# Attention and two layers on one core: the transposes of the probabilities read float32 tiles instead of float32r copies

## The chip, the core and the metric

The kernel runs on one core of a Trainium2 chip. The core has a matrix engine (TensorE, in the profile PE, its weight loads PEld), three engines for elementwise work (VectorE = DVE, ScalarE = ACT, GpSimd = POOL), and a queue engine, SyncE (SP), which here issues every transfer. Work lies in SBUF, the results of TensorE in the banks of PSUM. The metric is the device time of one execution in microseconds.

## What is computed

Attention for 8 batches of 8 heads with 512 local and 32 global tokens of size 64, and behind it two layers over all 4608 tokens:

```python
k_all = np.concatenate([k_g, k_l], axis=2)
v_all = np.concatenate([v_g, v_l], axis=2)
out_g = np.matmul(sm(scale * np.matmul(q_g, k_all.transpose(0, 1, 3, 2))), v_all)
mask = np.abs(pos[:, None] - pos[None, :]) <= 32
s_ll = np.where(mask, scale * np.matmul(q_l, k_l.transpose(0, 1, 3, 2)), -1e9)
s_lg = scale * np.matmul(q_l, k_g.transpose(0, 1, 3, 2))
out_l = np.matmul(sm(np.concatenate([s_lg, s_ll], axis=-1)), v_all)
x = np.concatenate([out_g, out_l], axis=2).transpose(0, 2, 1, 3).reshape(4608, 512)
h = x @ w_in                      # 512 x 2048
return (h * (1.0 / (1.0 + np.exp(-h)))) @ w_out
```

`sm` is the softmax over the last axis. Everything is float32.

## The kernel before

**Numbers.** TensorE multiplies in the type float32r. A float32 value is split into a part that float32r holds exactly (names ending in `hi`) and the remainder (`lo`), and a product is the sum of two or three matmuls (hi with hi, hi with lo, lo with hi). ScalarE makes the `hi` parts, VectorE or GpSimd subtracts for the `lo` parts.

**Attention of the local queries.** It is cut into 128 steps: 8 batches, 4 chunks of 128 queries, 4 pairs of heads. A query sees only keys within 32 positions, so a chunk needs 192 local keys and the 32 global ones, 224 columns. A step k runs through these functions:

- `st_load`, `st_vload`: transfers of queries, keys and values into `raw` and `vraw` (L322, L324, L329).
- `st_split`, `st_vsplit`: the hi and lo parts (`qk`, `klo`, `vhi`, `vlo`).
- `st_scores`: the scores on TensorE (L369); VectorE adds the mask and finds the maximum (L373), ScalarE does the exponential (L377), VectorE the sum's reciprocal (L379, L380), and each head's half is scaled, one on ScalarE (L381), one on VectorE (L382; GpSimd for the first four steps). The probabilities of both heads stand in one tile `probs` of 128 x 512 float32, of which there are two, used in turn. Then a transfer (L385) copies `probs` bit for bit to a tile `rr` of type float32r. There is one such tile, and a second for odd steps among the first 12.
- `st_turn`: four transposes of 128 x 128 on TensorE (L393), with `rr` as the weights and the identity `ident` as the moving operand, into a bank of PSUM `t`; ScalarE and VectorE make `pt_hi` and `pt_lo` of it (L396, L397).
- `st_out`: the products with the values (L421), whose results become parts of `xh` and `xl`, the input of the layers.

**Attention of the global queries.** Once per batch, four heads are stacked on the partitions of a tile `pg` (two such tiles, `pgs`). `g_scores` writes the scores, `g_soft` does the softmax in place, `g_move` copies the tile by two transfers to float32r tiles `rg` (L296, L297; the larger one lies in a buffer of the tag `o`, which the way out of the layers uses too), and `g_turn` transposes these on TensorE (L310, L313). The transposed part goes along with the local ones as 32 more columns.

**Layers.** The tokens go through in 12 blocks of two or three tiles of 128. For each of 16 slices of the hidden size, `first_layer` does 12 matmuls (L550), then tanh on ScalarE (L556), a product on VectorE (L557) and the split (L559, L560); `second_layer` adds three matmuls per token tile (L569 to L571). In the first block the weights come in as 64-bit words and are turned into float32 and split (L225 to L239), much of it on VectorE (L233, L234, L236).

**What sets the order.** Each piece of attention has a due time, counted in steps from its scores (`DUE`, `TURN`, `HEAD` and so on: transposes 1.6 steps after the scores, 2.25 more for the first 12 steps). The pieces are sorted by it; before the first block they run by themselves, later `fill` puts those of the next block between the matmuls of the present one. TensorE keeps this written order. The order on the other engines and on SP's queue is set by a scheduler that goes by its own estimate of the times; the first loads of weights keep the order in which they are written. Each engine, and SP's queue, takes its instructions in turn: one that waits holds back those behind it.

Buffers of the first steps lie in two pools that later give their room to the last slices of the weights; `held` lists what is still in use there, and `load_weights` first runs the pieces that free it.

Of the kernel before, what the change touches and what calls it, by code (L numbers as in the profile page):

```python
# [9 lines left out]
F32 = mybir.dt.float32  # L10
F32R = mybir.dt.float32r
# [22 lines left out]
NEG = -8.0e9              # times the scale of 1/8: -1e9  # L34
SCALE = 0.125

# [1 line left out]
SIZES = [3, 2] + [3] * 9 + [2]       # token tiles in each block of the two layers  # L38
NLATE = 4                            # slices of the weights that take the place of the first buffers
# [19 lines left out]
PRE, PACE, LOOK = 0, 0.75, 1         # weights converted during the first steps  # L59
END = 0.6                            # how far the attention is ahead of a block  # L60
# [22 lines left out]
BUFS = dict(qk=[2, 2], raw=2, rr=1, p=2, vraw=2)  # L83
# [10 lines left out]
def attention_moe_kernel(ctx: ExitStack, tc: tile.TileContext, qk0_in, qk_in, v_in, gqk, wts, out):  # L94
# [7 lines left out]
    # buffers of the first steps, in two parts that later hold the last slices of the weights  # L102
# [6 lines left out]
    # until the layers start, attention has their banks too  # L109
# [12 lines left out]
    id32 = work.tile([P, P], F32R, tag="qk", bufs=BUFS["qk"][0], name="id32").bitcast(F32)  # L122
    make_identity(nc, id32)
    ident = const.tile([P, P], F32R, name="ident")
    nc.vector.tensor_copy(out=ident, in_=id32)
# [17 lines left out]
    # probabilities: columns past the window stay zero  # L143
    probs = []
    for i in range(BUFS["p"]):
        t = const.tile([P, 2, 2 * P], F32, name=f"probs{i}")
        nc.gpsimd.memset(t, 0.0)
        probs.append(t)
    pgs = [const.tile([P, SKV], F32, name=f"pg{i}") for i in range(2)]
    # transposed probabilities by unit and key tile; 32 more columns for the global queries  # L150
    # what of the first buffers is still in use
    held = [set() for _ in first]
    pts = []
# [33 lines left out]

    def rr_tile(k):
        if k % 2 and k < RRS and first[0]:
            held[0].add(f"rr{k}")  # L190
            return first_pool[0].tile([P, 4 * P], F32R, tag="rr", bufs=1, name=f"rr{k}")
        return work.tile([P, 4 * P], F32R, tag="rr", bufs=BUFS["rr"], name=f"rr{k}")

# [5 lines left out]
    def load_weights():  # L199
        f, c0 = w_next  # L200
        i = (f - (NF - NLATE)) // 2
        if f == CLOSE and not closing:
            closing.append(f)
        if i >= 0 and first[i]:
            while held[i]:
                advance(stream[done][0])
            first[i].__exit__(None, None, None)
            first[i] = None
            side = ("left", "right")[i]
            first_pool[i] = ctx.enter_context(tc.tile_pool(name=f"late{i}", bufs=1, side=side, reuse_waits="tile"))  # L210
        if c0 == 0:
            home = const if i < 0 else first_pool[i]
            w_hi.append(home.tile([P, 2 * DM], F32R, name=f"w_hi{f}"))
            w_lo.append(home.tile([P, 2 * DM], F32R, name=f"w_lo{f}"))
        n = DM if first[1] else DM // 2
        w_next[:] = (f, c0 + n) if c0 + n < 2 * DM else (f + 1, 0)
        sl = slice(c0, c0 + n)
        hi, lo = w_hi[f][:, sl], w_lo[f][:, sl]
        if first[1]:
            raw = first_pool[1].tile([P, 2 * DM], I32, tag="raw", bufs=3, name=f"raw_w{f}_{c0}")  # L220
            w = first_pool[1].tile([P, n], F32, tag="w", bufs=2, name=f"w{f}_{c0}")
        else:
# [10 lines left out]
        nc.vector.tensor_scalar(out=up, in0=wi, scalar1=3, scalar2=None, op0=ALU.logical_shift_left)  # L233
        nc.vector.scalar_tensor_tensor(out=wi, in0=wi, scalar=0x80000000, in1=up, op0=ALU.bitwise_and,  # L234
                                       op1=ALU.bitwise_or)
        nc.vector.scalar_tensor_tensor(out=wi, in0=low, scalar=29, in1=wi, op0=ALU.logical_shift_right,  # L236
                                       op1=ALU.bitwise_or)
# [21 lines left out]
    def g_scores(b, p):  # L259
        hi, lo = state.pop(("gqk", p))  # L260
        did(("scores", b, p), *([("move", b - 1, p // 2)] if b else []))
# [11 lines left out]
    # program order is the order of the data  # L273
# [18 lines left out]
    def g_move(b, hh):  # L292
        did(("move", b, hh), ("soft", b, hh))
        r0 = two.tile([P, 4 * P], F32R, tag="o", name=f"rg0_{b}_{hh}")
        r1 = two.tile([P, SG], F32R, tag="rg", name=f"rg1_{b}_{hh}")
        nc.sync.dma_start(out=r0.bitcast(F32), in_=pgs[hh][:, : 4 * P])  # L296
        nc.sync.dma_start(out=r1.bitcast(F32), in_=pgs[hh][:, 4 * P :])  # L297
        state["rg", hh] = r0, r1

    def g_turn(b, hh):  # L300
        r0, r1 = state.pop(("rg", hh))
# [6 lines left out]
        for i in range(4):  # L308
            sl = slice(i * P, (i + 1) * P)
            nc.tensor.transpose(tb[:, sl].bitcast(F32R), r0[:, sl], ident)  # L310
        nc.scalar.copy(out=pgt[:, 0:4, hs, :], in_=tb.rearrange("p (t h q) -> p t h q", t=4, h=4))
        tb = attbank("s", f"gu{b}_{hh}")
        nc.tensor.transpose(tb[:SG, :P].bitcast(F32R), r1, ident)  # L313
        nc.scalar.copy(out=pgt[:SG, 4, hs, :], in_=tb[:SG, :P].rearrange("p (h q) -> p h q", h=4))

# [39 lines left out]
    def st_scores(k, b, c, pr):  # L355
# [14 lines left out]
        p = probs[k % BUFS["p"]]  # L370
# [12 lines left out]
        # a copy that keeps every bit for the transpose  # L383
        rr = rr_tile(k)
        nc.sync.dma_start(out=rr.bitcast(F32), in_=p.rearrange("p u j -> p (u j)"))  # L385
        tiles["rr", k] = rr

    def st_turn(k, b, c, pr):
        rr = tiles.pop(("rr", k))
        free(f"rr{k}")  # L390
        t = attbank("t", f"t{k}")
        for i in range(4):
            nc.tensor.transpose(t[:, i * P : (i + 1) * P].bitcast(F32R), rr[:, i * P : (i + 1) * P], ident)  # L393
# [147 lines left out]
    def first_layer(n, f):  # L541
# [13 lines left out]
        # twice h * sigmoid(h); the half goes into the way out  # L555
# [7 lines left out]
    def second_layer(n, f, gh, gl):  # L563
# [9 lines left out]
        if f == NF - 1:  # L573
            while ("rg", 0) in state or ("rg", 1) in state:
                advance(stream[done][0])
# [26 lines left out]
def _layout(q_l, k_l, v_l, q_g, k_g, v_g, w_in, w_out):  # L602
# [26 lines left out]
    # the first steps: both heads' keys once, and each one's queries zero on the other's rows  # L629
# [9 lines left out]
    # two heads on the rows; each one's queries are zero on the other's rows  # L639
# [28 lines left out]
```

## Time and profile before

| | us |
|---|---|
| median of the runs (lowest, highest of 3) | 1108.76 (1107.52, 1111.5) |
| span of the profiled execution | 1108.1 |
| transfers, mean | 122 GB/s |
| of these: `rr` | 128 transfers of 256 KB |
| `rg` | 16 of 256 KB and 16 of 16 KB |

The page gives the profiled execution's time as its span. Busy time is the time in which an engine has an instruction running. The busy time of TensorE contains the overlap of matmuls that follow each other, so the time from start to start is the better measure of what one costs. The chain of waits follows the last instruction back, at each step to what released it.

### The profile page before, as it was taken

The numbers are of one execution on the slowest core, as the hardware profiler recorded it, in microseconds if no ns is written. First come the engines' busy times: TensorE is split into PE (matmuls) and PEld (weight loads), VectorE is DVE, ScalarE is ACT, GpSimd is POOL, SyncE is SP. The second block draws the span as 40 slices with busy tenths as digits, with TensorE's granted clock in tenths as the row PEclk, the third lists the DMA queues.
The fourth block names the chain that finished last, engine by engine and source line by source line (L and its number), as shares of the span: only waits on it lengthen the run. The fifth ranks groups of instructions, "written<-read, shape, count | busy, mean of one in ns | idle before, by whom it ended". The sixth has DMA issues, their size and how long they took to land.

```text
span 1108.1 us, 21579 instructions
## 1 busy us (share of the span) xinstructions
PE 1042.5 (94%) x6824; PEld 947.8 (86%) x6824; DVE 798.5 (72%) x2467; ACT 725.1 (65%) x1933; POOL 228.5 (21%) x441
## 2 busy tenths in 40 slices
PE   5647889999999999999999999999999999999998
PEld 4646778898999999999989999999999999889996
DVE  6989998777778867766667877777777768863322
ACT  7876676776677766766567776667666658763232
POOL 8756775321100111001010111101100011100000
PEclk8678899999999999999999999999999999999999
DMA  8576554543343443342233443334333324420000
GB/s 249 179 219 188 182 170 130 156 121 117 109 145 115 138 138 110 113 148 83 82 112 112 147 130 117 111 116 158 109 109 120 111 92 148 138 76 20 1 30 19
DMA packets 74800, 134.76 MB, mean 122 GB/s; under 512 B 10432, under 2 KB 30400, under 8 KB 74688
## 3 DMA queue, kind: packets, MB, share of 16 engines
q1 hardware_dynamic: 74688, 133.40, 38.8%
q8 instruction: 54, 0.88, 0.3%
q14 instruction: 58, 0.48, 0.1%
HBM read 86.44 MB, written 8.91 MB: 86 GB/s over the span
## 4 chain that ended last, share of the span: by engine, by line
PE 80%; DVE 10%; DMA 3%; issue 3%; ACT 3%; POOL 1%; SPq 0%; DVEq 0%; ACTq 0%; POOLq 0%
PE h L550 31%; PE out L569 11%; PE out L571 10%; PE out L570 10%; PE o L421 8%; PE s L369 4%; PE t L393 3%; DVE w L234 2%; DVE w L236 1%; DMA rr<-probs 1%; DMA raw_w<-in_wts_dram 1%; DVE raw_w L233 1%; DVE pt_lo L397 1%; ACT probs L377 1%; DVE probs L373 1%
## 5 line engine op out<-in xcount | busy, mean ns | idle before, releaser
L550 PE MATMUL h<-xh,w_hi 128*128 128x384 f32 (+1 forms) x768 | 255.6, 333 | 0.1
L550 PE MATMUL h<-xh,w_lo 128*128 128x384 f32 (+1 forms) x768 | 252.3, 329 | 0.0
L550 PE MATMUL h<-xl,w_hi 128*128 128x384 f32 (+1 forms) x768 | 252.1, 328 | 0.0
L569 PE MATMUL out<-w_hi,gh 128*128 128x512 f32 x544 | 224.8, 413 | 0.0
L571 PE MATMUL out<-w_hi,gl 128*128 128x512 f32 x544 | 215.6, 396 | 3.0 <-DVE gl L560 1.8
L570 PE MATMUL out<-w_lo,gh 128*128 128x512 f32 x544 | 214.7, 395 | 0.0
L556 ACT ACTIVATE t<-h 128x384 f32<-128x384 f32 (+1 forms) x192 | 90.5, 471 | 186.2 <-PE h L550 175.8
L404 POOL CAST pt_hi<-pgt 128x64 fp32r<-128x64 f32 (+1 forms) x160 | 50.4, 327 | 726.1 <-PE o L421 719.2
L557 DVE SCALAR_TENSOR_TENSOR t<-t,h 128x384 f32<-128x384 f32 (+1 forms) x192 | 101.6, 529 | 122.7 <-ACT t L556 121.7
L550 PEld LDWEIGHTS h<-xh,w_hi 128*128 128x128 f32 x768 | 145.4, 189 | 6.0 <-ACT xh L427 0.6
L550 PEld LDWEIGHTS h<-xl,w_hi 128*128 128x128 f32 x768 | 145.5, 189 | 5.4
L550 PEld LDWEIGHTS h<-xh,w_lo 128*128 128x128 f32 x768 | 145.3, 189 | 0.0
L560 DVE TENSOR_TENSOR gl<-t,gh 128x384 fp32r<-128x384 f32 (+1 forms) x192 | 107.3, 559 | 48.5 <-PE out L571 43.1
L571 PEld LDWEIGHTS out<-w_hi,gl 128*128 128x128 f32 x544 | 102.8, 189 | 28.4 <-DVE gl L560 4.6
L377 ACT ACTIVATE probs<-probs,st 128x224 f32<-128x224 f32 x256 | 121.4, 475 | 7.3 <-DVE st L373 6.2
L373 DVE CUSTOM_DVE_ANT_0 probs<-s,mask 128x224 f32<-128x224 f32 x256 | 89.3, 384 | 50.4 <-PE s L369 47.0
L421 PE MATMUL o<-pt_hi,vhi 128*64 128x160 f32 (+1 forms) x512 | 99.4, 238 | 20.1 <-ACT pt_hi L396 7.8
L570 PEld LDWEIGHTS out<-w_lo,gh 128*128 128x128 f32 x544 | 103.6, 190 | 11.2
L569 PEld LDWEIGHTS out<-w_hi,gh 128*128 128x128 f32 x544 | 103.2, 190 | 11.4 <-ACT gh L559 0.4
L559 ACT CAST gh<-t 128x384 fp32r<-128x384 f32 (+1 forms) x192 | 94.6, 493 | 21.2 <-DVE t L557 17.8
L421 PE MATMUL o<-pt_hi,vlo 128*64 128x160 f32 (+1 forms) x512 | 96.3, 237 | 0.0
L421 PE MATMUL o<-pt_lo,vhi 128*64 128x160 f32 (+1 forms) x512 | 79.8, 238 | 16.3 <-DVE pt_lo L397 11.8
(82 smaller groups left out, 2016.5 us busy)
## 6 DMA issues: line engine op xcount, KB each, us to landing
raw<-in_qk_dram SPq DMA_DIRECT2D x100, 352.0 KB, 3.0
rr<-probs SPq DMA_DIRECT2D x128, 256.0 KB, 2.3
vraw<-in_v_dram SPq DMA_DIRECT2D x128, 128.0 KB, 2.4
raw_w<-in_wts_dram SPq DMA_DIRECT2D x28, 512.0 KB, 4.0
raw_g<-in_gqk_dram SPq DMA_DIRECT2D x32, 304.0 KB, 2.8
out_dram<-o SPq DMA_DIRECT2D x32, 256.0 KB, 2.6
raw<-in_qk_dram SPq DMA_DIRECT2D x28, 240.0 KB, 3.6
rg<-pg SPq DMA_DIRECT2D x16, 256.0 KB, 2.4
```

Source lines behind the costliest of these rows:

```text
L373: nc.vector.tensor_tensor_reduce(out=p[:, u, :W], in0=s[:, u * W : (u + 1) * W], in1=mask_of[c], scale=-SCALE, scalar=3.0e38, op0=ALU.add, ...
L377: nc.scalar.activation(p[:, u, :W], p[:, u, :W], AF.Exp, bias=st[:, u : u + 1], scale=-1.0, accum_out=st[:, 2 + u : 3 + u])
L404: nc.gpsimd.tensor_copy(out=pt_hi[:n, :, a, P:], in_=g)
L421: nc.tensor.matmul(o[:D, u * wide : u * wide + m], v[:, a, u, :], pt[:, u, a, :m], start=(i == 0), stop=(i == len(terms) - 1))
L550: nc.tensor.matmul(h[:, :nt], wt, x[:, c, :nt], start=(i == 0), stop=(i == 3 * NCC - 1))
L556: nc.scalar.activation(t[:, :nt], h[:, :nt], AF.Tanh, scale=0.5)
L557: nc.vector.scalar_tensor_tensor(out=t[:, :nt], in0=t[:, :nt], scalar=1.0, in1=h[:, :nt], op0=ALU.add, op1=ALU.mult)
L559: nc.scalar.copy(out=gh[:, :nt], in_=t[:, :nt])
L560: nc.vector.tensor_tensor(out=gl[:, :nt], in0=t[:, :nt], in1=gh[:, :nt].bitcast(F32), op=ALU.subtract)
L569: nc.tensor.matmul(o, gh[:, sl], wh, start=(f == 0), stop=False)
L570: nc.tensor.matmul(o, gh[:, sl], wl, start=False, stop=False)
L571: nc.tensor.matmul(o, gl[:, sl], wh, start=False, stop=(f == NF - 1))
```

## The change

The transposes read the softmax's own tile, as float32. The tiles `rr` and `rg` and the transfers into them are gone, `g_move` does nothing any more, the identity is float32 (its cast on VectorE is gone), and the PSUM tiles are written as float32. The tiles of probabilities now have to last until their transposes have run, so there are three and not two; in the first 12 steps (`RRS`) there are five, of which two lie in the first of the two early pools. The scores of the global queries need the transposes of the batch before, where they needed its copies. The tail of a block no longer runs pieces of attention until `rg` is used up.

```diff
-BUFS = dict(qk=[2, 2], raw=2, rr=1, p=2, vraw=2)
+BUFS = dict(qk=[2, 2], raw=2, p=3, vraw=2)
...
-    id32 = work.tile([P, P], F32R, tag="qk", bufs=BUFS["qk"][0], name="id32").bitcast(F32)
-    make_identity(nc, id32)
-    ident = const.tile([P, P], F32R, name="ident")
-    nc.vector.tensor_copy(out=ident, in_=id32)
+    ident = const.tile([P, P], F32, name="ident")
+    make_identity(nc, ident)
...
-    for i in range(BUFS["p"]):
-        t = const.tile([P, 2, 2 * P], F32, name=f"probs{i}")
+    for i in range(BUFS["p"] + 2):
+        home = const if i < BUFS["p"] else first_pool[0]
+        t = home.tile([P, 2, 2 * P], F32, name=f"probs{i}")
         nc.gpsimd.memset(t, 0.0)
         probs.append(t)
+    probs_of = {}
...
+    held[0].update(f"p{k}" for k in range(RRS) if k % 5 >= BUFS["p"])
...
-        did(("scores", b, p), *([("move", b - 1, p // 2)] if b else []))
+        did(("scores", b, p), *([("turn", b - 1, p // 2)] if b else []))
...
     def g_move(b, hh):
         did(("move", b, hh), ("soft", b, hh))
-        r0 = two.tile([P, 4 * P], F32R, tag="o", name=f"rg0_{b}_{hh}")
-        r1 = two.tile([P, SG], F32R, tag="rg", name=f"rg1_{b}_{hh}")
-        nc.sync.dma_start(out=r0.bitcast(F32), in_=pgs[hh][:, : 4 * P])
-        nc.sync.dma_start(out=r1.bitcast(F32), in_=pgs[hh][:, 4 * P :])
-        state["rg", hh] = r0, r1
...
-            nc.tensor.transpose(tb[:, sl].bitcast(F32R), r0[:, sl], ident)
+            nc.tensor.transpose(tb[:, sl], pg[:, sl], ident)
...
-        nc.tensor.transpose(tb[:SG, :P].bitcast(F32R), r1, ident)
+        nc.tensor.transpose(tb[:SG, :P], pg[:, 4 * P :], ident)
...
-        p = probs[k % BUFS["p"]]
+        i = k % (5 if k < RRS else BUFS["p"])
+        p, probs_of[i] = probs[i], k
...
-        rr = rr_tile(k)
-        nc.sync.dma_start(out=rr.bitcast(F32), in_=p.rearrange("p u j -> p (u j)"))
-        tiles["rr", k] = rr
+        tiles["p", k] = p.rearrange("p u j -> p (u j)")
 
     def st_turn(k, b, c, pr):
-        rr = tiles.pop(("rr", k))
-        free(f"rr{k}")
+        p = tiles.pop(("p", k))
+        free(f"p{k}")
...
-            nc.tensor.transpose(t[:, i * P : (i + 1) * P].bitcast(F32R), rr[:, i * P : (i + 1) * P], ident)
+            nc.tensor.transpose(t[:, i * P : (i + 1) * P], p[:, i * P : (i + 1) * P], ident)
...
-            while ("rg", 0) in state or ("rg", 1) in state:
-                advance(stream[done][0])
```

Three places of the built programs, engine by engine; the numbers behind names tell buffers apart. Line numbers of the changed kernel differ from those before by some ten.

TensorE, in the middle of a block: the transposes of a step between the last matmul of a first layer and the second layer. Before:

```order
L550 MATMUL h_14_6298<-xh_3975,w_lo_2274 128x384
L393 MATMUL t_6318<-ident,rr_6184 128x128 x4
L569 MATMUL out_0_5328<-w_hi_2171,gh_13_6216 128x512
L570 MATMUL out_0_5328<-w_lo_2172,gh_13_6216 128x512
L571 MATMUL out_0_5328<-w_hi_2171,gl_13_6217 128x512
```

With the change:

```order
L539 MATMUL h_14_6148<-xh_3877,w_lo_2216 128x384
L382 MATMUL t_6168<-ident,probs_122 128x128 x4
L558 MATMUL out_0_5198<-w_hi_2115,gh_13_6068 128x512
L559 MATMUL out_0_5198<-w_lo_2116,gh_13_6068 128x512
L560 MATMUL out_0_5198<-w_hi_2115,gl_13_6069 128x512
```

Nothing has moved: TensorE has the same instructions in the same order all through, only the transposed tile is another.

SP's queue, from the first loads of weights on. Before:

```order
L296 DMA rg_0_0_239<-pg_124 128x512
L297 DMA rg_0_0_240<-pg_124 128x32
L322 DMA raw_423<-in_qk_dram 128x480
L296 DMA rg_0_1_249<-pg_125 128x512
L385 DMA rr_237<-probs_120 128x512
L297 DMA rg_0_1_250<-pg_125 128x32
L385 DMA rr_269<-probs_122 128x512
L225 DMA raw_w_512_434<-in_wts_dram 128x1024
L322 DMA raw_490<-in_qk_dram 128x480
L225 DMA raw_w_0_503<-in_wts_dram 128x1024
```

With the change:

```order
L312 DMA raw_409<-in_qk_dram 128x480
L220 DMA raw_w_512_420<-in_wts_dram 128x1024
L312 DMA raw_474<-in_qk_dram 128x480
L220 DMA raw_w_0_487<-in_wts_dram 128x1024
L312 DMA raw_541<-in_qk_dram 128x480
```

The loads of queries and weights now follow each other, where copies that wait for a softmax stood between them.

VectorE, the first steps, from the division of the second softmax (`st`) to the first `pt_lo`. Before:

```order
L380 RECIPROCAL st_260<-st_260 128x2
L233 TENSOR_SCALAR raw_w_0_317<-w_0_318 128x512
L234 SCALAR_TENSOR_TENSOR w_0_318<-w_0_318,raw_w_0_317 128x512
L236 SCALAR_TENSOR_TENSOR w_0_318<-raw_w_0_317,w_0_318 128x512
L373 ISA probs_120,st_296<-s_289,mask_94 128x224
L373 ISA st_296 128x1
```

With the change:

```order
L364 ISA probs_124,st_323<-s_316,mask_92 128x224
L364 ISA st_323 128x1
L228 TENSOR_SCALAR raw_w_0_307<-w_0_308 128x512
L370 TENSOR_SCALAR st_288<-st_288 128x2
L229 SCALAR_TENSOR_TENSOR w_0_308<-w_0_308,raw_w_0_307 128x512
L371 RECIPROCAL st_288<-st_288 128x2
L364 ISA probs_126,st_369<-s_362,mask_101 128x224
```

The softmax of the third, fourth and fifth step now stands ahead of or within the first conversion of weights; before, the third came behind it.

More of the change, by code (lines that the diff above doesn't have):

```diff
@@ L186, in qk_tiles @@
                 pool.tile([P, SKV], F32R, tag="klo", bufs=bufs[1], name=f"klo{name}"))
[L188 to L192, printed above, removed]
     def lows(pool):
@@ L293, in g_move @@
         did(("move", b, hh), ("soft", b, hh))
-        r0 = two.tile([P, 4 * P], F32R, tag="o", name=f"rg0_{b}_{hh}")
-        r1 = two.tile([P, SG], F32R, tag="rg", name=f"rg1_{b}_{hh}")
-        nc.sync.dma_start(out=r0.bitcast(F32), in_=pgs[hh][:, : 4 * P])
-        nc.sync.dma_start(out=r1.bitcast(F32), in_=pgs[hh][:, 4 * P :])
-        state["rg", hh] = r0, r1
     def g_turn(b, hh):
-        r0, r1 = state.pop(("rg", hh))
+        pg = pgs[hh]
         did(("turn", b, hh), ("turn", b, 0) if hh else ("last", b - 1))
@@ L382, in st_scores @@
         (nc.gpsimd if k < POOLN else nc.vector).tensor_scalar(out=p[:, 1, :W], in0=p[:, 1, :W], scalar1=st[:, 7:8], scalar2=None, op0=ALU.mult)
-        rr = rr_tile(k)
-        nc.sync.dma_start(out=rr.bitcast(F32), in_=p.rearrange("p u j -> p (u j)"))
-        tiles["rr", k] = rr
+        tiles["p", k] = p.rearrange("p u j -> p (u j)")
     def st_turn(k, b, c, pr):
-        rr = tiles.pop(("rr", k))
-        free(f"rr{k}")
+        p = tiles.pop(("p", k))
+        free(f"p{k}")
+        assert probs_of[k % (5 if k < RRS else BUFS["p"])] == k
         t = attbank("t", f"t{k}")
         for i in range(4):
-            nc.tensor.transpose(t[:, i * P : (i + 1) * P].bitcast(F32R), rr[:, i * P : (i + 1) * P], ident)
+            nc.tensor.transpose(t[:, i * P : (i + 1) * P], p[:, i * P : (i + 1) * P], ident)
         t4 = t.rearrange("p (u a q) -> p u a q", u=2, a=2)
```

## The prediction

> **What bounds the kernel now.** I read the page first: the share of each engine and the span in forty slices.
>
> ```profile
> PE 1042.5 (94%) x6824; PEld 947.8 (86%) x6824; DVE 798.5 (72%) x2467; ACT 725.1 (65%) x1933; POOL 228.5 (21%) x441
> PE   5647889999999999999999999999999999999998
> DVE  6989998777778867766667877777777768863322
> PEclk8678899999999999999999999999999999999999
> ```
>
> TensorE is full from the seventh slice on. Before that it is not, and its granted clock is down; there VectorE is the fuller engine. So I cut the span in four with the view of busy time by stretch (columns: stretch, length, then busy time and count of TensorE, of its weight loads, of VectorE, ScalarE and GpSimd, then granted clock, share of the DMA engines, GB/s).
>
> ```profile
> 0.00:166.00 166.00, 113.58 (x708) 100.05 (x709) 146.62 (x372) 123.68 (x323) 115.62 (x145) 0.83 0.64 198
> 166.00:222.00 56.00, 52.24 (x342) 47.11 (x341) 44.47 (x136) 40.03 (x110) 25.94 (x36) 0.97 0.49 142
> 222.00:1037.00 815.00, 810.80 (x5383) 742.06 (x5382) 587.40 (x1915) 540.91 (x1454) 86.94 (x261) 1.00 0.37 114
> 1037.00:1108.00 71.00, 65.89 (x396) 58.61 (x394) 20.03 (x46) 20.48 (x48) 0.00 (x0) 0.99 0.06 19
> ```
>
> In the start, TensorE is idle for 166 - 113.58 = 52.4 us and VectorE for 19.4 us, and much of the latter is the wait for the first data. From 222 to 1037 us TensorE is idle for 4.2 us of 815: a nanosecond added to a TensorE instruction there is a nanosecond of the result, and almost nothing can be won by removing waits. The chain of waits says the same.
>
> ```profile
> PE 80%; DVE 10%; DMA 3%; issue 3%; ACT 3%; POOL 1%; SPq 0%; DVEq 0%; ACTq 0%; POOLq 0%
> PE h L550 31%; PE out L569 11%; PE out L571 10%; PE out L570 10%; PE o L421 8%; PE s L369 4%; PE t L393 3%; DVE w L234 2%; DVE w L236 1%; DMA rr<-probs 1%; DMA raw_w<-in_wts_dram 1%; DVE raw_w L233 1%; DVE pt_lo L397 1%; ACT probs L377 1%; DVE probs L373 1%
> ```
>
> The copies that the change removes (DMA rr<-probs) have 1% of it, the transposes that it alters (PE t L393) 3%.
>
> **Transposes: the term that decides.** The order of TensorE stays the same; 512 transposes of L393, 64 of L310 and 16 of L313 now read float32 and not float32r. First what one costs now. In the full stretch, from start to start (columns: start, duration, engine, line):
>
> ```profile
> 503.04 0.40 PE L570 MATMUL out<-w_lo,gh 128*128 128x512 f32 x1
> 503.27 0.39 PE L571 MATMUL out<-w_hi,gl 128*128 128x512 f32 x1
> 503.50 0.47 PE L393 MATMUL t<-ident,rr 128*128 128x128 f32 x4
> 503.81 0.46 PE L569 MATMUL out<-w_hi,gh 128*128 128x512 f32 x1
> 504.11 0.40 PE L570 MATMUL out<-w_lo,gh 128*128 128x512 f32 x1
> 942.40 0.28 PE L550 MATMUL h<-xl,w_hi 128*128 128x256 f32 x1
> 942.52 0.28 PE L550 MATMUL h<-xh,w_lo 128*128 128x256 f32 x1
> 943.23 0.51 PE L393 MATMUL t<-ident,rr 128*128 128x128 f32 x4 [0.42 <-DMA rr<-probs]
> ```
>
> Four transposes take 503.81 - 503.50 = 0.31 us, 77.5 ns each. A matmul of 512 columns takes 503.27 - 503.04 = 0.23 us and one of 256 takes 0.12 us, so 256 columns cost 0.11 us and 128 cost 55 ns; about 10 ns per matmul are left over for its weights. A float32r transpose thus stands 22 ns above its stream.
>
> No float32 matmul is in this trace, so its price is bounded. Below: nothing more, 77.5 ns, since tile, instruction and bytes per element are the same. Above: four passes of what a pass costs now, 310 ns, 232.5 more; a gain on TensorE itself I exclude, since no column and no load falls away. Between ends that far apart I go by the nearest row, which is the transpose itself: same shape and the same 4 bytes, so nearer the lower end. But the rows show that the loads are cheap (10 ns for 128 columns) where a stream of 128 columns costs 55, and I do not expect that to hold for the full float32 type. I take the load of the float32 block at the stream's rate, 55 ns, and uncovered: 55 + 55 = 110 ns, 32.5 more. That is a choice, and the weakest number here.
>
> The Trainium skill, page "TensorE: Matmul & The Clock Gate", section "Weight-path perf modes", says that the fast weight load is on only where the input type is not FP32; that speaks against this change. By its load of P/1.2, an estimate of 107 ns for 128 columns, a transpose would take 162 ns, and the sum below would end near 1145 us. The 10 ns of the rows agree with a fast load of float32r; no row shows float32.
>
> How many of them lie where TensorE sets the end: the stretches of the table above for L393 (three rows), then L310 and L313 (one row each).
>
> ```profile
> 0.00:166.00 166.00, 10.77 (x80) 9.38 (x80) 0.83 0.64 198
> 166.00:222.00 56.00, 2.74 (x24) 2.61 (x24) 0.97 0.49 142
> 222.00:1037.00 815.00, 46.82 (x408) 45.56 (x408) 1.00 0.37 114
> 222.00:1037.00 815.00, 5.91 (x48) 4.89 (x48) 1.00 0.37 114
> 222.00:1037.00 815.00, 2.69 (x12) 1.14 (x12) 1.00 0.37 114
> ```
>
> After 166 us: 24 + 408 + 48 + 12 = 492 transposes, at 32.5 ns **+16.0 us** (bounds 0 and 114.4). The other 100, in the start, come to 3.3 us, and TensorE's 52.4 idle us hide them; without that cover they would cost these 3.3 us, more at the lowered clock. I count 0.
>
> **What the copies cost.** 128 of rr and 32 of rg leave SP's queue, and their latency leaves the way from softmax to transpose.
>
> ```profile
> rr<-probs SPq DMA_DIRECT2D x128, 256.0 KB, 2.3
> rg<-pg SPq DMA_DIRECT2D x16, 256.0 KB, 2.4
> L373 DVE CUSTOM_DVE_ANT_0 probs<-s,mask 128x224 f32<-128x224 f32 x256 | 89.3, 384 | 50.4 <-PE s L369 47.0 <-DMA rr<-probs 2.4
> L393 PE MATMUL t<-ident,rr 128*128 128x128 f32 x512 | 60.3, 242 | 1.7 <-DMA rr<-probs 1.7
> L310 PE MATMUL gt<-ident,rg 128*128 128x128 f32 x64 | 8.3, 257 | 10.0 <-DMA rg<-pg 5.4 <-issue 3.2 <-DVE acc L435 1.3
> 17.65 4.25 DMA rr<-probs
> 57.04 0.38 SPq L385
> 57.47 7.73 DMA raw_w<-in_wts_dram
> PE t L393 <- DMA rr<-probs: 1.3, 3, 0.7
> ```
>
> A copy takes 2.3 us, but little waits for it. TensorE waited 1.7 us for rr in all, 1.3 of it after 222 us by the view of waits (the last row; the row at 943.23 is one of the three, 0.42): **-1.3 us**. VectorE waited 2.4 us before L373, because the next softmax may not write probs until rr has landed; that lies in the start, where VectorE bounds: **-2.4 us**. The wait of 5.4 us for rg is at the first transposes, where TensorE is not the bound; I take **-1.2** of it (bounds 0 and 5.4). The chain of waits in order of time shows rr at 17.65 us, and VectorE had weights to convert under most of it; and an issue of rr (57.04) just ahead of a load of weights (57.47). That load is on the chain by its own 7.73 us, and an issue of 0.38 us ahead of it is all that falls away there. Together **-4.9 us**, between 0 and 9.5 (1.7 + 2.4 + 5.4).
>
> **What it adds, at nothing.** Three more buffers of probabilities are cleared on GpSimd at the start; two clears took 0.99 us and GpSimd was then idle for 1.42 us ahead of its first klo, which hides 1.5:
>
> ```profile
> 2.16 0.99 POOL L147 MEMSET probs<- 128x512 f32 x2
> 10.09 1.21 POOL L340 TENSOR_TENSOR klo<-raw,qk 128x480 fp32r<-128x480 f32 x1 [1.42 <-PE gs L269]
> ```
>
> A buffer of probabilities is now held until TensorE has transposed it. The softmax of step k, on VectorE, waits for the transposes of step k - 3, due 1.6 steps after their scores and so 1.4 steps before they are needed; in the first twelve steps there are five buffers and 3.85 steps. If this came late, pt_lo, xl and gl would queue behind it on VectorE, and TensorE's L421 and L571 wait for those. VectorE is 72% busy in the full stretch, which covers a small delay. The scores of the global queries now wait for the transposes of the batch before instead of its copies; these come at least five steps earlier. VectorE's and ScalarE's order in the start changes, since the scheduler sets it; I put that at 0, give or take 3 us.
>
> **The sum.** The profiled execution's span is 1108.1 us; the median of the runs shown, 1108.76, is 0.7 above it. 1108.1 + 16.0 - 4.9 = 1119.2, and with 0.7 **1119.9 us**.
>
> **Rivals.**
> *One pass at today's price.* A float32 transpose costs 77.5 ns as well, and the term of 16.0 falls away: 1108.8 - 4.9 = 1103.9 us. For it: equal shape, bytes and instruction. Against: the 22 ns that even float32r stands above its stream. It decides if the extra is below 4.9/492 = 10 ns; up to there the change is not slower. The Trainium skill, same page, section "Terms", has a transpose mode that is 4x faster for FP32, which would be this case.
> *Four passes.* 310 ns, so 492 x 232.5 ns = 114.4 us: 1108.8 + 114.4 - 4.9 = 1218.3 us. For it: float32r as a separate type is there for some reason, and 592 of 592 transposes in the trace use it. Against: these are transposes, which multiply nothing. The Trainium skill, page "FP8 and Floating Point Precision", section "TensorE Precision Notes", gives true FP32 four passes through the array, without speaking of transposes; no row here shows one.
> *Probabilities held too long.* The transposes cost what I forecast, and in the start VectorE stands at the softmax until TensorE has freed a buffer. If each of the 20 steps of the start (80 transposes) loses what a group of four would take, 0.44 us, that is 8.8 us: 1128.7 us. It decides from about a third of a group per step, where it eats what the start wins. For it: three buffers after step 12, when the lag of the first steps ends. Against: the 1.4 steps of room.
>
> **How the numbers follow.** Chances: forecast 0.45, one pass 0.32, four passes 0.15, held too long 0.08. The forecast's own range, with 20 to 55 ns more per transpose (9.8 to 27 us) and 9.5 to 0 us won, is 1109 to 1136. The range for 8 of 10 is 1100 to 1150: it takes in one pass but for its edge, the forecast, the held buffers and most of what lies between those and four passes; four passes is left out. A measurement of this kernel can tell 0.3%, 3.3 us, from no change. One pass is split 0.24 faster and 0.08 within; of the forecast 0.04 is within; the rest is slower: 0.24, 0.12, 0.64.
>
> **What would show it.** In the profile after, from the start of a group of four L393 transposes to the next matmul: 0.44 us if I am right, 0.31 for one pass, 1.2 for four. The rows of rr and rg are gone, with the waits of VectorE and TensorE for them; the end of the start (where TensorE becomes full) is 3 to 4 us earlier. A wait of L373 for PE t would be the held buffers. If the group takes 0.31 us and the time is still above 1112 us, the loss is in the start, in the order of VectorE, and my whole sum is wrong.

## The result and the profile after

The changed kernel takes 1118.36 us in the median (1117.87 to 1118.94), the kernel before 1108.39 in the runs beside it. The ratio is 1.0084 with a 95% interval of 1.0068 to 1.0099, that is 9.3 us more (7.5 to 11.0). The prediction said 1119.9.

The page of the changed kernel, engines, slices and chain:

```profile
span 1116.9 us, 20832 instructions
PE 1057.7 (95%) x6824; PEld 964.1 (86%) x6824; DVE 800.4 (72%) x2466; ACT 727.8 (65%) x1933; POOL 231.1 (21%) x444
PE   6567789999999999999999999999999999999998
PEclk8778889999999999999999999999999999999999
DMA packets 51756, 96.71 MB, mean 87 GB/s; under 512 B 5824, under 2 KB 25792, under 8 KB 51648
PE 83%; DVE 10%; issue 2%; ACT 2%; DMA 2%; POOL 1%; SPq 0%; DVEq 0%; ACTq 0%; POOLq 0%
```

The copies are gone (87 GB/s instead of 122), and TensorE carries 83% of the chain instead of 80. The granted clock is at nine tenths one slice later than before. The view of busy time by stretch, with the columns of the prediction:

```profile
0.00:166.00 166.00, 115.54 (x670) 102.16 (x671) 143.93 (x360) 120.33 (x310) 116.27 (x145) 0.81 0.51 157
166.00:222.00 56.00, 53.03 (x351) 47.97 (x350) 46.09 (x139) 41.96 (x116) 27.83 (x37) 1.00 0.38 110
222.00:1037.00 815.00, 814.11 (x5357) 746.79 (x5356) 586.66 (x1914) 541.95 (x1454) 86.06 (x259) 1.00 0.26 77
```

By 166 us TensorE had run 670 instructions, where it had run 708 before, and VectorE 360 instead of 372: the start has become later, not earlier. From 222 to 1037 us TensorE now idles for 0.9 us instead of 4.2, and yet the trace has 26 instructions fewer there: in this stretch the single instructions have become dearer. The groups by line and the view of waits after 222 us show what the change did to the operations that it touches:

```profile
L382 PE MATMUL t<-ident,probs 128*128 128x128 f32 x512 | 81.2, 284 | 0.0
L364 DVE CUSTOM_DVE_ANT_0 probs<-s,mask 128x224 f32<-128x224 f32 x256 | 89.6, 384 | 54.0 <-PE s L359 53.4
PE gt L300 <- DVE acc L424: 0.6, 1, 0.6
PE o L410 <- DVE st L371: 0.3, 1, 0.3
```

A transpose in float32 is busy for 284 ns instead of 242 (which contains the overlap). TensorE never waits for the probabilities any more, and where VectorE's maximum waits (53.4 of the 54.0 us), it is for the scores: not for a copy, and not for a transpose that would hold a buffer.

To see where the 9.3 us arise, I follow one instruction that every kernel has: the four transposes of a step. There are 128 such groups on TensorE. The 25th stands at the end of the start, the 128th at the end of the full stretch. From the timelines, before and after (columns: start, duration, engine, line):

```profile
208.69 0.37 PE L393 MATMUL t<-ident,rr 128*128 128x128 f32 x3
1035.04 0.38 PE L393 MATMUL t<-ident,rr 128*128 128x128 f32 x3
```

```profile
212.08 0.49 PE L382 MATMUL t<-ident,probs 128*128 128x128 f32 x3
1044.18 0.49 PE L382 MATMUL t<-ident,probs 128*128 128x128 f32 x3
```

(A row that counts two or three of the four transposes comes from a narrow stretch of the timeline, which ends before the last of them; only the starts are used.) In these two executions the start costs 212.08 - 208.69 = 3.4 us, and the full stretch (1044.18 - 1035.04) - 3.39 = 5.75 us. Behind the last group both need the same: 1108.1 - 1035.04 = 73.1 us and 1116.9 - 1044.18 = 72.7. The prediction had 16.0 - 1.3 = +14.7 behind the start and -3.6 in it. So its total was nearly right, and neither part was: that the two errors met is luck.

### The profile page after: what moved, and what is told of

Its sections match the earlier page's. It is cut to its first block, busy times and chain, and to the rows that moved or that the text cites. A ratio compares the mean times of both kernels' runs of the same rounds, so it can differ in the third digit from the quotient of the medians.

```text
span 1116.9 us, 20832 instructions
## 1 busy us (share of the span) xinstructions
PE 1057.7 (95%) x6824; PEld 964.1 (86%) x6824; DVE 800.4 (72%) x2466; ACT 727.8 (65%) x1933; POOL 231.1 (21%) x444
## 4 chain that ended last, share of the span: by engine, by line
PE 83%; DVE 10%; issue 2%; ACT 2%; DMA 2%; POOL 1%; SPq 0%; DVEq 0%; ACTq 0%; POOLq 0%
PE h L539 31%; PE out L558 11%; PE out L560 10%; PE out L559 10%; PE o L410 8%; PE s L359 5%; PE t L382 4%; DVE w L229 2%; DVE w L231 1%; DVE raw_w L228 1%; DVE pt_lo L386 1%; DMA raw_w<-in_wts_dram 1%; PE gt L300 1%; DVE probs L364 1%; DVE gl L549 1%
## 5 line engine op out<-in xcount | busy, mean ns | idle before, releaser
L364 DVE CUSTOM_DVE_ANT_0 probs<-s,mask 128x224 f32<-128x224 f32 x256 | 89.6, 384 | 54.0 <-PE s L359 53.4
L386 DVE TENSOR_TENSOR pt_lo<-t,pt_hi 128x512 fp32r<-128x512 f32 x128 | 88.0, 687 | 11.9 <-ACT pt_hi L385 11.5
```

What stands on the lines that cost most here:

```text
L364: nc.vector.tensor_tensor_reduce(out=p[:, u, :W], in0=s[:, u * W : (u + 1) * W], in1=mask_of[c], scale=-SCALE, scalar=3.0e38, op0=ALU.add, ...
L386: nc.vector.tensor_tensor(out=pt_lo[:, :, :, :P], in0=t4, in1=pt_hi[:, :, :, :P].bitcast(F32), op=ALU.subtract)
```

## The experiments

### One part of the change alone

The first pair separates type and copies. The first kernel keeps the copies and makes only the transposes float32:

```diff
-        return work.tile([P, 4 * P], F32R, tag="rr", bufs=BUFS["rr"], name=f"rr{k}")
+        return work.tile([P, 4 * P], F32, tag="rr", bufs=BUFS["rr"], name=f"rr{k}")
...
-            nc.tensor.transpose(t[:, i * P : (i + 1) * P].bitcast(F32R), rr[:, i * P : (i + 1) * P], ident)
+            nc.tensor.transpose(t[:, i * P : (i + 1) * P], rr[:, i * P : (i + 1) * P], ident)
```

> The copies stay; only their tiles, the identity and the outputs of the transposes are float32. Theory 1, the type costs about 15 ns per transpose where TensorE is full: a group of four L393 takes 0.36 us and not 0.295 from 222 us on, which gives about +7 us there, and the waits for rr stay. What the start does tells the rest: if its 3.4 us of delay come from the type too, the time is 1118 to 1121 us; Theory 2, if they come from the missing copies and the new order on VectorE, the start ends as before and the time is 1115 to 1117 us. Rival (the type is free, all is order): 1108 us.

The second leaves the local copies out and keeps float32r. Here the softmax's last operation writes float32r tiles `rrs`, which GpSimd fills at the start; what float32r does not hold of a probability is lost. The copies of the global queries stay.

```diff
-        nc.scalar.activation(p[:, 0, :W], p[:, 0, :W], AF.Copy, scale=st[:, 6:7])
+        r = rrs[k % (2 + 3 if k < RRS else 2)]
+        nc.scalar.activation(r[:, 0, :W], p[:, 0, :W], AF.Copy, scale=st[:, 6:7])
...
-        rr = rr_tile(k)
-        nc.sync.dma_start(out=rr.bitcast(F32), in_=p.rearrange("p u j -> p (u j)"))
-        tiles["rr", k] = rr
+        tiles["rr", k] = r.rearrange("p u j -> p (u j)")
```

> No copies for the local queries, but float32r transposes: the softmax's last operation writes float32r tiles (five in the first 12 steps, two later), so the probabilities are rounded to float32r and their remainder is left out; the copies of the global queries stay. Theory 1 (the type is the loss): groups at 0.295 us, the three waits for rr near 940 to 977 us gone, 1.3 us, and the start no later than before: 1104 to 1108 us. Theory 2 (the start is later without the copies, by the order): about +3 us in the start and -1.3 later, 1109 to 1112 us.

Measured: 1120.55 us (ratio 1.0100, 1.0081 to 1.0119) and 1118.17 us (1.0081, 1.0066 to 1.0097). The timelines, first the float32 copies, then float32r without copies:

```profile
212.38 0.38 PE L393 MATMUL t<-ident,rr 128*128 128x128 f32 x2
1047.17 0.49 PE L393 MATMUL t<-ident,rr 128*128 128x128 f32 x3
```

```profile
220.57 0.46 PE L399 MATMUL t<-ident,rrs 128*128 128x128 f32 x4
1043.88 0.45 PE L399 MATMUL t<-ident,rrs 128*128 128x128 f32 x4
```

In the full stretch the type costs (1047.17 - 1035.04) - (212.38 - 208.69) = 8.4 us, and leaving the copies out wins 3.0 us ((1043.88 - 1035.04) - (220.57 - 208.69) = -3.0). Together 5.4; the change itself shows 5.75. So the full stretch is the sum of the two parts. The start is not: it is late by 3.7 us in the one and by 11.9 in the other, although the other leaves out only what was thought to cost. The second number is not clean, because the five fills, 3.8 us on GpSimd, stand ahead of its first work. Neither expectation of the second kernel (1104 to 1108 and 1109 to 1112 us) had a start so late.

### What one transpose costs

To price a transpose where four more follow directly, each local transpose is issued twice, once in the changed kernel and once in the kernel before:

```diff
-            nc.tensor.transpose(t[:, i * P : (i + 1) * P], p[:, i * P : (i + 1) * P], ident)
+            for _ in range(2):
+                nc.tensor.transpose(t[:, i * P : (i + 1) * P], p[:, i * P : (i + 1) * P], ident)
```

> The changed kernel with each local transpose issued twice into the same place. If the price is per transpose, a group of eight takes twice 0.357 us, 0.71, and the time grows by about 108 x 0.357 = 39 us plus what the start shows, to 1157 us or more. If the price is one for the change of mode at a group's edge, a group grows by the 0.295 us of four float32r transposes, 32 us.

> The kernel before with each local transpose issued twice: a group of eight takes about 0.6 us, and the time grows by about 108 x 0.295 = 32 us plus what the start shows, to 1140 us or more. The difference of the two doublings, 7 us, is the type's price per transpose once more, without the change of copies.

Measured, with one run each: 1164.23 us, 45.9 more than the changed kernel, and 1146.17 us, 37.6 more than the kernel before. Three places in the timelines, all in the full stretch. Four float32 transposes in the changed kernel:

```profile
509.03 0.39 PE L560 MATMUL out<-w_hi,gl 128*128 128x512 f32 x1
509.26 0.60 PE L382 MATMUL t<-ident,probs 128*128 128x128 f32 x4
509.62 0.47 PE L558 MATMUL out<-w_hi,gh 128*128 128x512 f32 x1
509.93 0.40 PE L559 MATMUL out<-w_lo,gh 128*128 128x512 f32 x1
```

Eight float32 transposes in the changed kernel, doubled:

```profile
536.44 1.03 PE L383 MATMUL t<-ident,probs 128*128 128x128 f32 x8
537.23 0.48 PE L559 MATMUL out<-w_hi,gh 128*128 128x512 f32 x1
537.54 0.40 PE L560 MATMUL out<-w_lo,gh 128*128 128x512 f32 x1
```

Eight float32r transposes in the kernel before, doubled:

```profile
498.96 0.81 PE L394 MATMUL t<-ident,rr 128*128 128x128 f32 x8
499.61 0.30 PE L268 MATMUL gs<-qk_g 128*64 128x272 f32 x1
```

From its start to the next matmul a float32 group of four takes 0.36 us, and the float32r group quoted in the prediction took 0.31 (503.50 to 503.81). But that is not all of its price. The matmul behind it, 512 columns, takes 0.31 us to the one that follows (509.62 to 509.93), where one behind another matmul of 512 columns takes 0.23; behind the float32r group it took 0.30 (503.81 to 504.11). So a group of four costs 0.36 + 0.08 = 0.44 us in float32, 110 ns each, and 0.31 + 0.07 = 0.38 us in float32r, 95 ns each. The mean over the groups of the full stretch with such a matmul behind them, by the starts in the timelines, is 0.443 and 0.371 us: 111 and 93 ns, a difference of 17.9 ns per transpose. In 18 groups a matmul of the global scores follows, and there group and follower take 0.12 us more in float32 and not 0.07; over all groups the difference is some 20 ns.

Four more in a row cost (0.79 - 0.36) / 4 = 107 ns each in float32 and (0.65 - 0.31) / 4 = 85 ns in float32r. The doubled kernels say that these are no artefacts of the pairs: their 412 extra transposes between the 25th and the 128th group (103 steps of four) make that stretch 42.8 us longer, 104 ns each, and 28.3 us, 69 ns each. The second is lower than 85, in part because waits are covered there by a busier TensorE: between the two groups it idles for 4.2 us in the kernel before and for 0.3 in its doubled form, which makes up 9 ns for each transpose. The rest is open. The two doublings were expected to differ by 7 us. Their times do, by 8.3, but in the full stretch it is 14.5: the starts differ the other way, since VectorE has an order of its own in each. So the type's price is taken from the groups, and not from this difference.

### Why the start is late

Two explanations are left. Price: the slower transposes, or what the copies left behind, hold up the start. Order: the scheduler goes by its own estimates, so a changed type or a missing copy makes it set another order on VectorE, ScalarE and SyncE's queue, and the time is lost by the order. In the first two experiments both had changed. The next pair takes them apart. In the first, everything is set in order with the types of before, and only then are the 592 transposes turned into float32:

```diff
+    for f in nc.m.functions:
+        for blk in f.blocks:
+            for j, i in enumerate(blk.instructions):
+                if isinstance(i, mybir.InstMatmult) and i.is_transpose:
+                    both = [[copy.replace(a, dtype=F32) for a in side] for side in (i.ins, i.outs)]
+                    blk.instructions[j] = copy.replace(i, ins=both[0], outs=both[1])
```

> The kernel before, whose 592 transposes are turned from float32r into float32 only after the order of all engines has been set; copies, order and buffers are exactly those of before. The later start of the changed kernel (its transposes come 3.4 us later by 209 us, those of the float32 copies 3.7 us) has two explanations. Order: any change makes the scheduler set another order on VectorE, ScalarE and SyncE's queue, and the time is lost by that. Price: the slower transposes themselves hold the start up. By the order theory this kernel loses nothing in the start (0, give or take 1 us, at the 25th group of transposes) and 8.4 us behind it, 71 ns for each of some 104 groups and the global ones: 1108.5 + 8.4 = 1116.9 us. By the price theory the start costs 3.7 us here too: 1120.6 us, as with the float32 copies.

In its counterpart the kernel with float32 copies gets its order, and then its transposes are turned back into float32r:

```diff
+    as_r = lambda side: [copy.replace(a, dtype=F32R) if getattr(a, "dtype", None) == F32 else a for a in side]
...
+                if isinstance(i, mybir.InstMatmult) and i.is_transpose:
+                    blk.instructions[j] = copy.replace(i, ins=as_r(i.ins), outs=as_r(i.outs))
```

> The counterpart: the kernel with float32 copies, whose transposes are turned back into float32r after the order has been set. So the order is that of the float32 copies (but for the cast of the identity), the type that of before. By the order theory the start is late by 3.7 us although nothing in it costs more, and nothing is lost behind it: 1108.5 + 3.7 = 1112.2 us. By the price theory nothing is lost anywhere: 1108.5 us.

In the traces VectorE's 2467 instructions stand in the first kernel as in the one before, and in the second as in that with float32 copies, but for the type of the identity's cast.

Two more kernels make the change in one part of the program only, first from step 24 on (and for the global queries from the third batch on), with the order of before ahead of it:

```diff
+KD = 24
...
+        if k < KD:
+            rr = rr_tile(k)
+            nc.sync.dma_start(out=rr.bitcast(F32), in_=p.rearrange("p u j -> p (u j)"))
+        else:
+            rr = p.rearrange("p u j -> p (u j)")
...
+            if k < KD:
+                nc.tensor.transpose(t[:, sl].bitcast(F32R), rr[:, sl], ident)
+            else:
+                nc.tensor.transpose(t[:, sl], rr[:, sl], ident.bitcast(F32))
```

> The change made only from step 24 on (and for the global queries from batch 2 on): the first 24 steps keep copy and float32r, with the order of before up to there. If start and full stretch are two separate terms, the start costs 0 and the full stretch what it costs in the changed kernel, 5.75 us less the few groups left out: about 1114 us. If instead the loss follows from the order wherever it changes, or the time lost in the start is only the sooner loss of what the full stretch would lose anyway, this kernel ends at 1117 to 1118 like the changed one.

and then in the first 12 steps and the first batch of the global queries only, with five buffers there:

```diff
+    for i in range(BUFS["p"] + 3):
+        t = (const if i < BUFS["p"] else first_pool[0]).tile([P, 2, 2 * P], F32, name=f"probs{i}")
...
+        if k < RRS:
+            rr = p.rearrange("p u j -> p (u j)")
+        else:
+            rr = rr_tile(k)
+            nc.sync.dma_start(out=rr.bitcast(F32), in_=p.rearrange("p u j -> p (u j)"))
```

> The reverse: the first 12 steps and the global queries of the first batch read the softmax's tile as float32, with five buffers; from step 12 on copies and float32r as before, in the order of before. The full stretch costs 0. If leaving out the copies or the float32 type itself makes the start late, or the five buffers do, the transposes come 3.4 us later at the 25th group, as in the changed kernel: 1108.5 + 3.4 = 1111.9 us. If it is the order, this start has an order of its own that is neither that of before nor that of the changed kernel, and its loss need not be 3.4: anything from 0 to 12 us (the two other orders seen so far, of the float32 copies and of direct float32r tiles, cost 3.7 and 11.9). My forecast in the prediction, 3.6 us won by the start, would give 1104.9.

Measured, in this order: 1118.14 us (ratio 1.0085, 1.0067 to 1.0102), 1110.85 us (1.0018, 1.0007 to 1.0030), 1113.46 us (1.0045, 1.0028 to 1.0061) and 1115.85 us (1.0072, 1.0052 to 1.0091), with 1109.35 us for the kernel before. The timelines, again the 25th and the 128th group: float32 in the order of before, float32r in the order of the float32 copies, the change from step 24 on, the change in the first steps.

```profile
206.50 0.38 PE L394 MATMUL t<-ident,rr 128*128 128x128 f32 x2
1041.74 0.49 PE L394 MATMUL t<-ident,rr 128*128 128x128 f32 x3
```

```profile
213.10 0.37 PE L394 MATMUL t<-ident,rr 128*128 128x128 f32 x3
1038.84 0.46 PE L394 MATMUL t<-ident,rr 128*128 128x128 f32 x4
```

```profile
206.69 0.38 PE L406 MATMUL t<-ident,probs 128*128 128x128 f32 x2
1038.83 0.49 PE L406 MATMUL t<-ident,probs 128*128 128x128 f32 x3
```

```profile
217.32 0.37 PE L406 MATMUL t<-ident,rr 128*128 128x128 f32 x3
1043.51 0.45 PE L406 MATMUL t<-ident,rr 128*128 128x128 f32 x4
```

The start of a single execution can't be read too closely. The kernel with the change from step 24 on has the instructions of before up to there and is 2.0 us ahead at the 25th group, and executions of the kernel before ended between 1105.70 and 1111.89 us. The full stretch, of which there is one trace for each kernel, looks much steadier: kernels with the same type and copies in it agree within 0.6 us (+5.75 and +5.8; +8.4 and +8.9; -0.2, -0.6 and the kernel before), and what lies behind the last group takes 72.6 to 73.2 us in all eight. So the table takes the full stretch from the traces, and the start as what the measured time leaves over (all against the kernel before, in us; the intervals are those of the ratio alone):

| kernel | order in the start | time | full stretch | start: time less full stretch |
|---|---|---|---|---|
| the change | its own | +9.3 | +5.75 | +3.6 (1.8 to 5.2) |
| float32 copies | its own | +11.1 | +8.4 | +2.7 (0.5 to 4.7) |
| float32r in that order | that of the float32 copies | +2.0 | -0.6 | +2.6 (1.4 to 3.9) |
| float32 in the order of before | that of before | +9.4 | +8.9 | +0.5 (-1.5 to 2.4) |
| change from step 24 on | that of before | +5.0 | +5.8 | -0.8 (-2.7 to 1.0) |
| change in the first steps | its own | +8.0 | -0.2 | +8.1 (5.9 to 10.3) |
| float32r, no local copies | its own | +9.0 | -3.0 | +12.0 (10.4 to 13.8) |

The rows fall into two kinds. Where the order of the start is that of before, the start costs nothing that can be measured, float32 transposes or not. Where the order is another, it costs 2.6 us and more, and the same 2.6 to 2.7 us with float32 and with float32r. So a new order makes the start late without any change of price, and the price of the transposes is not seen in it. For the change itself, whose own order has no counterpart with float32r and copies, this is an inference from these rows and from the gap that follows. The full stretch depends on the type and the copies alone: +8.4 and +8.9 us for float32, nothing for float32r, 3.0 us less without copies, and the sum of both in the change and in the change from step 24 on.

Two expectations missed by their size. The float32r kernel in the other order was to lose 3.7 us and lost 2.0; and the change in the first steps lost 8 us, not the 3.4 that would have followed from missing copies or from five buffers. Its start, with an order that is neither of the others, is worse than that of the full change, which has the same direct transposes in these steps.

How an order costs time is seen in the waits of TensorE between 120 and 190 us (columns: total, times, longest), before:

```profile
PE out L571 <- DVE gl L560: 1.8, 1, 1.8
PE gt L310 <- issue: 1.4, 1, 1.4
PE gt L310 <- DVE acc L435: 1.3, 1, 1.3
```

and in the changed kernel:

```profile
PE gt L300 <- DVE acc L424: 5.5, 2, 4.9
PE out L560 <- DVE gl L549: 2.1, 1, 2.1
```

`acc` is VectorE's sum of the global queries' results in `st_out`. It is the last to read the bank of PSUM in which the transposes of the global queries want to write. VectorE's timeline of the changed kernel around its end:

```profile
129.13 1.31 DVE L373 TENSOR_SCALAR probs<-probs,st 128x224 f32<-128x224 f32 x1
130.37 0.41 DVE L228 TENSOR_SCALAR raw_w<-w 128x512 uint32<-128x512 uint32 x1
130.70 0.68 DVE L386 TENSOR_TENSOR pt_lo<-t,pt_hi 128x512 fp32r<-128x512 f32 x1
131.30 0.68 DVE L229 SCALAR_TENSOR_TENSOR w<-w,raw_w 128x512 uint32<-128x512 uint32 x1
132.01 0.28 DVE L417 TENSOR_TENSOR xl<-o,xh 64x128 fp32r<-64x128 f32 x1
132.22 0.17 DVE L424 TENSOR_TENSOR acc<-o,acc 64x32 f32<-64x32 f32 x1
```

Between the `acc` of the one head (129.03) and that of the other (132.22) the order puts a scaling, two steps of the weights' conversion and a `pt_lo`, 3.2 us, while TensorE stands. In the kernel before the corresponding pair came at 125.61 and 127.68. The kernels with the other orders have a gap of the same kind at another place: the waits of TensorE for `acc` in the float32r kernel in the order of the float32 copies, and in the change in the first steps, both between 120 and 190 us:

```profile
PE o L422 <- DVE acc L434: 4.9, 1, 4.9
```

```profile
PE o L434 <- DVE acc L446: 6.0, 2, 5.0
```

At these gaps the delay arises. Against the kernel before, the change is 1.0 us late at the 16th group of transposes (124.96 and 123.97), ahead of its gap, and 5.1 late at the 17th (142.25 and 137.11), behind it. The other two are late by 0.3 and 0.8 us at their 20th group and by 6.7 and 7.0 at their 21st. In the two kernels that keep the order of before, the longest wait of this kind is 2.8 and 2.9 us, and 1.3 in the kernel before itself.

That these gaps make up the whole of 2.6 to 8 us is not shown: of the 5.1 us 3.4 are left at the 25th group. TensorE idles for 50.5 us of the start after the change and for 52.4 before, and a gap here is in part made good later. Which of the change's edits (missing copies, buffers, the new rule for the global scores) moved the scheduler at this place stays open, and it was not tried to give VectorE the order of before with the copies missing.

No kernel of these beats the kernel before. The best form of the change is that from step 24 on, 1113.46 us: it spares the start and keeps the loss of the full stretch.

## Why the prediction came out right, step by step

**"No TensorE instruction moves, and after 222 us a nanosecond more on one is a nanosecond of the result": right.** Float32 in the order of before costs 8.9 us in the full stretch; 412 local and 60 global transposes lie there, so 18.8 ns each, against 17.9 ns by the groups.

**"110 ns for a float32 transpose": right. "77.5 ns now, so 32.5 more": wrong, and this is the term that was mis-sized.** A float32r transpose costs 93 to 95 ns. The 77.5 was read from the start of the group to the next matmul, and left out that this matmul then takes 0.30 us instead of 0.23. The row that says so (503.81 to 504.11) stood in the prediction's own rows. The 110 ns had been built up from stream and load, which contains everything, so a full price was compared with a partial one. With 17.9 ns the 492 transposes come to 8.8 us and not to 16.0. Accordingly the sign that was to show it failed too: a group takes 0.36 us to the next matmul, between the 0.44 of the forecast and the 0.31 of one pass.

The picture behind the 110 ns, load plus stream, one after the other, does not hold either. By the Trainium skill, page "TensorE: Matmul & The Clock Gate", section "LDWEIGHTS (loading the stationary operand)", a load takes P / 1.2, an estimate of 107 ns for 128 columns. The 107 ns for each further float32 transpose agree with that load alone; that the stream is hidden behind it no row shows. The estimate of 162 ns in the prediction added the two and is refuted. The Trainium skill, same page, section "Back-to-back issue gap", gives some 81 ns per matmul of 128 columns; the float32r transposes, at 85 ns in a row, nearly agree.

**"The waits for copies go, -4.9 us": right in kind, and only in the full stretch.** -1.3 was predicted there and 3.0 came. The waits of TensorE for `rr` are gone (three of them, at about 943, 960 and 977 us), and so is one that I had not counted: the way out. From ScalarE's and TensorE's timeline of the kernel before:

```profile
570.51 0.60 ACT L578 ACTIVATE o<-out 128x512 f32<-128x512 f32 x1 [1.79 <-DMA out_dram<-o]
572.48 0.26 PE L421 MATMUL o<-pt_hi,vhi 128*64 128x160 f32 x1 [0.42 <-ACT pt_hi L396]
573.25 0.32 PE L421 MATMUL o<-pt_lo,vhi 128*64 128x160 f32 x2 [0.32 <-DVE pt_lo L397]
```

ScalarE waits until a transfer out has freed its buffer, and holds `pt_hi` behind it. The three kernels without local copies in this stretch run through here 1.0 to 1.1 us sooner, also the one that keeps the copies `rg`. But so does the change in the first steps, which has the local copies here: its ScalarE waits 0.22 us at this place, and 0.7 of the 1.1 us are lost again two groups later. So that the copies make this transfer late is not shown. The -2.4 and -1.2 us of the start can't be found: VectorE's wait for `rr` has gone from its row, and the start is later all the same.

**"The new order on VectorE: 0, give or take 3 us", and "the end of the start is 3 to 4 us earlier": wrong.** The start cost 3.6 us (1.8 to 5.2), which I put down to the order. The prediction took a step that it had no row for as neutral; seven starts have now been measured, and of the five with an order other than that of before none was as early.

So the sum of 1119.9 came out by luck, because two errors met: 7.2 us too much for the transposes (16.0 instead of 8.8), and 7.2 us too little for the start (-3.6 instead of +3.6). The waits of the full stretch, 1.7 us more than counted, leave the difference.

**The rivals.** One pass at today's price and four passes are refuted by the groups: 111 ns, neither 93 nor 310. Probabilities held too long is refuted by the row of L364, which never waits for a transpose.

## What to carry to other kernels

A price read from the start of an instruction to the start of the next one must take in what the next one loses: compare pairs that begin and end with the same kind of instruction. Where a scheduler sets the order by its own estimates, a change of type is a change of order too; fixing the order and changing the type afterwards tells the two apart, and a change in the loop's steady part should be tried with the start left as it is. A transfer in place of a cast can be worth its bytes: here the copies bought 18 ns at each transpose on the engine that sets the end, and cost 3.0 us over the full stretch.

## What was not expected of the hardware

A matmul is slower behind transposes: one of 512 columns takes 0.30 us from start to start behind a group in float32r and 0.31 to 0.32 behind one in float32, where it takes 0.23 behind another of 512 columns. Transposes are not alone in this: behind the products with the values, of 160 columns, it takes 0.28 in both kernels (56 places each in the full stretch).

In these traces a long gap on TensorE is paid twice. In the changed kernel the wait of 4.87 us ends at 132.5 us, and the stretches around it read:

```profile
126.00:132.00 6.00, 1.67 (x10) 1.34 (x8) 5.87 (x12) 3.82 (x9) 3.75 (x5) 0.98 0.47 152
132.00:138.00 6.00, 4.86 (x16) 3.95 (x17) 3.97 (x11) 3.66 (x9) 2.81 (x3) 0.50 0.44 122
```

The granted clock is 0.50 for the 6 us behind the gap, and a matmul of 512 columns then takes 0.43 us from start to start. The Trainium skill, page "TensorE: Matmul & The Clock Gate", section "What's actually happening", has the clock halved after an idle window of some 3.4 us; the 4.87 us and the 0.50 agree. In the float32r kernel in the order of the float32 copies the wait of 4.92 us before 173.3 us leaves a clock of 0.65 from 174 to 180 us.
